# Attention of the last two batches in chunks of 32 queries and 64 keys on quarters and eighths of the matrix array

## The chip, the core and the metric

The kernel runs on one core of a Trainium2 chip. The core has a matmul engine (PE, with its weight loads shown apart as PEld), three engines for elementwise work (DVE, ACT and POOL) and a queue engine SP that only issues transfers. Data lies in on-chip memory of 128 partitions; matmul results go to a second on-chip memory, the accumulator banks. Transfers run on 16 DMA engines, which SP, POOL and ACT feed through queues of their own (q1, q0 and q10 in the profile). The metric is device time in microseconds.

## What is computed

Four batches, 8 heads, 768 positions, 64 numbers per head. Attention works in chunks of 32 queries; each sees 8 memory keys of its head, its own 32 keys, 16 keys to the left and 8 to the right:

```python
for c in range(nc):                       # nc = 768 / 32 = 24
    l_start = max(0, c_start - 16); r_end = min(S, c_start + 32 + 8)
    k_full = concat([mem_k, k[:, :, l_start:r_end]]); v_full = concat([mem_v, v[...]])
    a = exp(q_c @ k_full.T / 8 - max); a = a / (sum(a) + 1e-9)
    out[:, :, c_start:c_end] = a @ v_full
x = out.transpose(0, 2, 1, 3).reshape(B, S, 512)
u = x + real(fft(fft(x, axis=1), axis=2))
un = (u - mean(u)) / sqrt(var(u) + 1e-6)
out = u + relu(un @ w_ch1) @ w_ch2        # 512 -> 2048 -> 512
```

So a chunk needs 8 + 16 + 32 + 8 = 64 keys.

## The kernel before

Each batch goes through three parts: attention (`attention`, two heads at a time, four pairs a batch, 16 pairs n = 0 to 15), a Fourier part with sums and statistics (`fourier`, `columns_of`), and an MLP (`mlp`, three blocks of 256 rows, each with a first layer L775 and a second layer L793; in batches 2 and 3 the second layer is made from seven half-size products, L842).

**Attention of a pair.** q and k come through POOL's queue with a cast to bf16 (`e_load_qk`, L345 and L349). For batches 0 to 2 PE turns them (L377) and ACT or DVE copies the result out (L395, L420). For batch 3 they are loaded row by row and turned by a DMA transpose from SP (`e_flip_q`, `e_flip_k`), and DVE copies windows of k from `kU` into `kTb` (L415). `kTb` holds 12 blocks of 128 columns: 32 empty ones, 8 memory keys (L408) and 88 keys around a block of 64 queries. Scores (L433) are made in two groups of six blocks; the two heads lie in the two row halves of the array:

```python
nc.tensor.matmul(sc[:, hh, t6, :], kT[r0:r0 + 64, t, :], qT[r0:r0 + 64, ts(t, 64)],
                 start=True, stop=True, tile_position=(r0, 0))
```

A block of 64 queries holds two chunks with different keys, so two exponentials per group (L441) add a bias `mbias` that removes the keys of the other chunk. The values `va` (L358, L362, L367: seven transfers by SP a pair) have the same 128-row blocks and a 65th column of ones, which gives the sum of the exponentials. Value matmuls (L457) are float32, two groups of 12, into two banks `xa` and `xo`; the two blocks of 64 queries lie in the two column halves of the array. A float32 matmul shows as two records. DVE divides by the sum (`e_norm`, L467 and L468) into the batch's buffer `xsb`, of which there are three; batch 3 uses batch 0's again.

**The order of the work.** Nothing is scheduled on the chip. `Plan.order` (L92) walks through a list of tasks while the program is built: each has an engine, a cost, predecessors (`after`, `behind`), buffers that it takes and gives back, and for transfers a size (`moved`, `grain`). It writes one fixed order for each engine. MLP tasks have the lowest priority and fill PE where nothing else is due. On the chip every engine and queue works in that order and waits where something is not ready. SP's queue carries the v loads, the turning of the Fourier rows through DRAM (L567, L568, read back by POOL, L572), the transposes of the MLP's input (`e_flip`, L748), those of batch 3's q and k, and the stores (L856, L859, L866).

## Time and profile before

| | |
|---|---|
| median of 3 runs | 281.31 us (281.21 to 281.39) |
| the profiled execution's own time | 282.55 us |
| its span, first to last instruction | 280.7 us |
| PE busy, granted clock | 264.3 us, 1.0 throughout |
| DVE, ACT, POOL busy | 193.5, 155.2, 64.3 us |
| scores: L433, 384 matmuls | 11.5 us on PE |
| values: L457, 768 records | 28.8 us on PE |
| exponentials: L441, 64 | 33.6 us on ACT, 0.576 us each |
| q and k loads of batch 3: 16 of 96 KB | 8.9 and 9.5 us from issue to landing |

A line of the profile names a source line, an engine, what is written and read, and how often. In a chain line the numbers are the start and the length of a piece, both in microseconds; "x12" counts matmuls, or records where a float32 matmul has two. PE's records overlap, since a matmul takes some 0.2 us from first to last number while the next starts earlier, so the length of a piece of many is read from the chain. Rows by stage give the stage, its length, the busy time of PE, PEld, DVE, ACT and POOL with their instructions, the granted clock, the mean busy share of the 16 DMA engines and GB/s.

### The profile page before, as it was taken

How to read it: one execution, taken by the hardware profiler on the slowest of the kernel's cores; microseconds unless marked ns; L12 is line 12 of the kernel's file. 1: busy time of each engine (PE TensorE's matmuls, PEld its weight loads, DVE VectorE, ACT ScalarE, POOL GpSimd, SP SyncE). 2: the span in 40 equal slices, each digit the busy share in tenths (PEclk: the TensorE clock that was granted, in tenths of full speed). 3: DMA queues.
4: the chain of work that ended last, by engine and by line, in shares of the span. 5: the costliest groups of instructions: out<-in, count | busy, mean ns of one | idle time of the engine just before them, and what ended most of it. 6: DMA issues, size and time to landing. Idle time of an engine off the chain costs nothing.

```text
span 280.7 us, 7981 instructions
## 1 busy us (share of the span) xinstructions
PE 264.3 (94%) x3325; PEld 207.4 (74%) x3325; DVE 193.5 (69%) x424; ACT 155.2 (55%) x262; POOL 64.3 (23%) x127
## 2 busy tenths in 40 slices
PE   0589999999999999998999999999999999999995
PEld 0466698788756579766668766858988888888884
DVE  7968978970218979899688776599869825353444
ACT  6887667579665757734745665525526270605150
POOL 8840853240111038306200230101004100000000
PEclk9999999999999999999999999999999999999999
DMA  6989999999899969999999734497101507103152
GB/s 102 199 143 174 162 206 204 196 198 201 162 190 236 214 103 220 177 142 144 235 191 209 177 74 109 108 207 167 48 37 58 131 21 168 40 37 77 50 103 76
DMA packets 116116, 39.98 MB, mean 142 GB/s; under 512 B 104560, under 2 KB 111472, under 8 KB 116080
## 3 DMA queue, kind: packets, MB, share of 16 engines
q1 hardware_dynamic: 93888, 23.54, 46.9%
q0 software_dynamic: 21472, 15.21, 34.0%
q10 hardware_dynamic: 720, 0.72, 0.7%
q8 instruction: 26, 0.43, 0.7%
q14 instruction: 10, 0.08, 0.1%
HBM read 37.36 MB, written 13.37 MB: 181 GB/s over the span
## 4 chain that ended last, share of the span: by engine, by line
PE 84%; DMA 7%; DVE 4%; SPq 3%; issue 1%; POOL 0%; POOLq 0%
PE ph L775 31%; PE pc L793 15%; PE pc L842 13%; DMA va<-in_v_dram 6%; PE ps L529 6%; PE xa L457 4%; PE pm L699 4%; PE ps L688 3%; PE xo L457 3%; PE sc L433 2%; SPq L358 2%; DMA qs<-in_q_dram 1%; PE trk L377 1%; PE trq L377 1%; DVE xsb L705 1%; PE pm L580 1%
## 5 line engine op out<-in xcount | busy, mean ns | idle before, releaser
L775 PE MATMUL ph<-unT,w_sb 128*128 128x256 f16 x768 | 90.3, 273 | 0.8 <-DVE xsb L800 0.8
L784 ACT ACTIVATE hT<-ph 128x512 f16<-128x512 f32 x96 | 56.9, 598 | 54.3 <-PE pc L842 30.2
L775 PEld LDWEIGHTS <-w_sb 128*128 128x128 f16 x768 | 73.2, 98 | 11.1 <-issue 1.7
L793 PE MATMUL pc<-w_sb,hT 128*128 128x512 f16 x192 | 44.8, 380 | 0.0
L441 ACT ACTIVATE e<-sc,mbias 128x384 f32<-128x384 f32 x64 | 33.6, 576 | 19.0 <-PE sc L433 19.0
L793 PEld LDWEIGHTS <-hT 128*128 128x128 f16 x192 | 17.7, 98 | 19.0 <-issue 0.2
L847 DVE TENSOR_TENSOR xsb<-pc,xsb 128x256 f32<-128x256 f32 x43 | 18.0, 421 | 12.4 <-PE pc L842 10.6
L842 PEld LDWEIGHTS <-hT 128*128 128x128 f16 x240 | 23.3, 98 | 4.2 <-DVE hT L830 1.0
L842 PE MATMUL pc<-w_sb,hT 128*128 128x256 f16 x192 | 24.1, 272 | 0.5 <-DVE hT L830 0.5
L541 ACT CAST up<-ps 128x386 f16<-128x386 f32 x16 | 9.7, 605 | 17.6 <-PE ps L529 17.0
L830 DVE TENSOR_TENSOR S<-hT 128x768 f16<-128x768 f16 (+1 forms) x12 | 5.1, 422 | 18.5 <-ACT hT L784 17.9
L800 DVE SCALAR_TENSOR_TENSOR xsb<-pc,rstd,xsb 128x512 f32<-128x512 f32 x12 | 9.0, 750 | 12.2 <-PE pc L793 12.1
L713 DVE BATCH_NORM_STATS2 st<-xsb 128x6 f32<-128x512 f32 x24 | 16.6, 690 | 0.6
L705 DVE TENSOR_TENSOR xsb<-pm,xsb 128x512 f32<-128x512 f32 x15 | 10.2, 678 | 7.1 <-PE pm L699 6.9
L457 PEld LDWEIGHTS xa<-va,e 128*64 128x64 f32 x384 | 12.5, 137 | 3.2 <-issue 2.0
L457 PE MATMUL xa<-va,e 128*64 128x65 f32 x384 | 14.7, 226 | 0.0
L433 PEld LDWEIGHTS <-kTb 64*128 64x128 bf16 x384 | 7.8, 96 | 9.0 <-issue 8.1
L457 PE MATMUL xo<-va,e 128*64 128x65 f32 x384 | 14.1, 223 | 0.0
L546 DVE TENSOR_TENSOR up<-ps,up 128x386 f16<-128x386 f32 x16 | 9.6, 602 | 6.1 <-ACT up L541 6.1
L395 ACT COPY qT<-trq 128x768 bf16<-128x768 bf16 x12 | 9.5, 793 | 6.4 <-PE trq L377 6.4
L572 POOL DMA_DIRECT2D xr<-x_back x3 | 2.3, 770 | 46.7 <-DMA x_back<-x_rows 46.7
L519 DVE TENSOR_TENSOR lo<-ff,hi 128x768 f16<-128x768 f32 x12 | 11.3, 954 | 2.4 <-ACT hi L514 2.4
(168 smaller groups left out, 455.3 us busy)
## 6 DMA issues: line engine op xcount, KB each, us to landing
va<-in_v_dram SPq DMA_DIRECT2D x32, 220.0 KB
w_sb<-in_moe_w_ch_dram POOLq DMA_DIRECT2D x8, 512.0 KB, 16.9
out_dram<-xsb SPq DMA_DIRECT2D x12, 256.0 KB
qs<-in_q_dram POOLq DMA_DIRECT2D x12, 192.0 KB, 6.5
ks<-in_k_dram POOLq DMA_DIRECT2D x12, 192.0 KB, 7.0
x_rows<-xsb POOLq DMA_DIRECT2D x3, 768.0 KB, 4.6
xr<-x_back POOLq DMA_DIRECT2D x3, 768.0 KB, 5.0
out_rows<-xsb SPq DMA_DIRECT2D x9, 256.0 KB
```

Of the source, the lines that this page charges most:

```text
L433: nc.tensor.matmul(sc[:, hh, t6, :], kT[r0:r0 + 64, t, :], qT[r0:r0 + 64, ts(t, 64)], start=True, stop=True, tile_position=(r0, 0))
L441: nc.scalar.activation(e1[:, :, :, ts(half, 32)], sc[:, :, 0:6, ts(half, 32)], AFT.Exp, bias=mbias[:, half:half + 1], scale=1.0 / math.sqr ...
L457: nc.tensor.matmul(xa[64 * half:64 * half + 64, st, hh, 0:65], e1[:, hh, t6, :], v1[:, hh, 6 * g + t6, 0:65], start=True, stop=True)
L519: nc.vector.tensor_tensor(lo[:, ab].rearrange(fl), ff_of[b, par][:, ab].rearrange(fl), hi[:, ab].rearrange(fl), ALU.subtract)
L529: nc.tensor.matmul(out_[:, sp, :], part[:, ab, sp * 3 + st, c0:c1], tab[:, sp, st, :], start=(st == 0 and i == 0), stop=(st == 2 and i == 1))
L705: nc.vector.tensor_tensor(uv, pm_of[b, kt], uv, ALU.add)
L713: nc.vector.bn_stats(st6, xs[b][:, kt, :])
L775: nc.tensor.matmul(ph[:, k, :], w1_sb[:, dt, ts(HH * k + i, P)], unT_of[b, j][:, dt, :], start=(dt == 0), stop=(dt == NDT - 1))
L784: nc.scalar.activation(hT_of[b, j][:, :, i, :], ph, AFT.Relu, bias=0.0, scale=1.0 if b in EVEN else -1.0)
L793: nc.tensor.matmul(pc_of[b, j, r], hT_of[b, j][:, k, i, ts(r, P)], w2_sb[:, HH * k + i, :], start=(i + k == 0), stop=(i + k == HH))
L842: nc.tensor.matmul(pc_of[key], a[:, i, :], w[:, i, :], start=(i == 0 and new), stop=(i == HH - 1), skip_group_check=not new)
L847: nc.vector.tensor_tensor(u, pc, u, ALU.add)
```

## The change

For pairs n >= 8 (batches 2 and 3) a chunk of 32 queries gets a block of its own with exactly its 64 keys, so the exponential needs no mask. `kTb` is then read as 24 blocks of 64 columns. Scores are 48 matmuls of 32 columns, each on one quarter of the array (64 rows by 64 columns): the row half is the head, the column half alternates with the chunk. Values are 48 float32 matmuls on eighths (64 rows by 32 columns): the row half is where the chunk's exponentials lie, the column quarter is the chunk's place in a tile of 128 queries, so the result comes out as 128 queries by 6 tiles for one head, one head in `xa` and one in the other bank. One exponential replaces four. The `va` buffers get the new layout: 12 transfers a pair, with the memory rows in both halves, and once for each of four buffers the ones column and empty edges are written again by ACT (`e_recast`), from a pattern that POOL makes at the start (`e_edge`).

Batch 3's q and k are cast once, whole, from DRAM to DRAM by two POOL transfers (`e_cast`), behind batch 1's read-back; SP then loads them in bf16 row by row (16 transfers).

The planner changes too: costs and transfer sizes of tasks are new; idle times of ACT and DVE overlap a little (`OVER`); SP holds back after a large transfer until 2.2 us before its end by the model (`ROOM`); dependencies of reused buffers are written out (`t_used`); and the list of tasks is ordered 25 times, 24 of them with ranks moved at random for tasks after the first Fourier part, keeping the order with the earliest modelled end (`shortest`). So the order of all engines' work differs, the first part aside. The loads of v for pairs 14 and 15 come behind batch 2's row turning.

```diff
+    OVER = {"DVE": 0.08, "ACT": 0.1}
+    lead = 0
+    ROOM = 2.2
...
+    def shortest(self, tries, spread):
+        free, ranks = dict(self.free), [t["rank"] for t in self.tasks]
+        found = None
+        for i in list(range(tries)) + [None]:
+            draw = random.Random(found[1] if i is None else i)
...
+                t["rank"] = rank if even or rank < self.lead or rank > 1e5 else rank + move
...
+            placed = self.order()
+            if found is None or self.end < found[0]:
+                found = (self.end, i)
+        return placed
...
-                if idle.get(e, 0.0) > now:
+                if idle.get(e, 0.0) > now or (e == "SP" and self.full and self.full["done"] - self.ROOM > now):
...
+    NCH = S // CHUNK
+    FINE = 8
...
+    def e_edge():
+        nc.gpsimd.memset(edge, 1.0)
+        for p0, hh, t, i in EDGES:
+            ones = edge[p0:p0 + 32, i:i + 1]
+            nc.gpsimd.affine_select(out=ones, in_=ones, compare_op=ALU.is_ge, fill=0.0, ...)
+            if i == 0:
+                nc.gpsimd.memset(edge[p0:p0 + NMEM, i:i + 1], 1.0)
+
+    def e_recast(i):
+        v1 = va[i]
+        nc.scalar.activation(v1[:, :, :, D], strided(mhalf, 0, [[0, 2], [0, NT]]), AFT.Copy, scale=-2.0)
+        for p0, hh, t, j in EDGES:
+            nc.scalar.copy(v1[p0:p0 + 32, hh, t, 0:D], zero[p0:p0 + 32].to_broadcast([32, D]))
+            nc.scalar.copy(v1[p0:p0 + 32, hh, t, D:D + 1], edge[p0:p0 + 32, j:j + 1])
...
+    half_qk = nc.dram_tensor("half_qk", [2, H, S, D], BF16).ap()
+
+    def e_cast(i):
+        rows = [x.rearrange("h s d -> (h s d)").rearrange("(e r c) -> e r c", e=16, c=2048)
+                for x in (half_qk[i], (q, k)[i][TURNED])]
+        nc.gpsimd.dma_start(*rows)
...
-                nc.gpsimd.dma_start(
+                nc.sync.dma_start(
                     strided(dst[n % NS], hh * D, [[2 * D, NST], [1, D]]),
-                    src[b, 2 * pr + hh].rearrange("(a p) d -> p a d", p=P))
+                    half_qk[i, 2 * pr + hh].rearrange("(a p) d -> p a d", p=P))
...
+        if n >= FINE:
+            for hh in range(2):
+                lo, hi = 64 * hh + NMEM, 64 - 64 * hh + NMEM
+                run(lo, WIN, 1, NT - 1, 64 - LEFT, hh)
+                run(hi, WIN, 0, NT - 1, CHUNK - LEFT, hh)
+                run(lo + LEFT, WIN - LEFT, 0, 1, 0, hh)
+                run(hi, WIN - RIGHT, NT - 1, 1, S - CHUNK - LEFT, hh)
+                for half in range(2):
+                    nc.sync.dma_start(v1[64 * half:64 * half + NMEM, hh, :, 0:D],
+                                      mem_v[b, 2 * pr + hh].unsqueeze(1).to_broadcast([NMEM, NT, D]))
+            return
...
+    def half_of(c, hh):
+        return 64 * ((c + hh) % 2)
+
+    def f_scores(n):
+        qT, kT = qT_of[n], kTb[n % NKT].rearrange("p t (h k) -> p (t h) k", h=2)
+        sc_of[n] = sc = aps.tile([P, 2, 16, CHUNK], FP32, tag="sc", bufs=1, name="sc")
+        for c in range(NCH):
+            for hh in range(2):
+                r0, p0 = 64 * hh, half_of(c, hh)
+                nc.tensor.matmul(sc[p0:p0 + 64, hh, c // 2, :], kT[r0:r0 + 64, c, :],
+                                 qT[r0:r0 + 64, ts(c, CHUNK)], start=True, stop=True,
+                                 tile_position=(r0, p0))
+
+    def f_exp(n):
+        sc = sc_of.pop(n)
+        e1_of[n] = e1 = apool.tile([P, 2, NT, CHUNK], FP32, tag="e1", bufs=3, name="e1")
+        nc.scalar.activation(e1, sc[:, :, 0:NT, :], AFT.Exp, scale=1.0 / math.sqrt(D))
+
+    def f_values(n):
...
+        for c in range(NCH):
+            for hh in range(2):
+                p0, c0 = half_of(c, hh), CHUNK * (c % 4)
+                nc.tensor.matmul(xa[hh][c0:c0 + CHUNK, c // 4, 0:65],
+                                 e1[p0:p0 + 64, hh, c // 2, :], v1[p0:p0 + 64, hh, c // 2, 0:65],
+                                 start=True, stop=True, tile_position=(p0, c0))
...
+        if n == TURNED * HP:
+            t_cast.extend(add("POOL", 1.0, lambda i=i: e_cast(i), moved=2.6, grain=0.2, late=1.0,
+                              behind=t_xr[1]) for i in range(2))
...
+        if FINE <= n < FINE + NV:
+            t_ones[n] = add("ACT", 1.0, lambda: e_recast(n % NV), [t_used.get(("va", n % NV)), t_edge, t_zero])
+        lv = add("SP", 2.5, lambda: e_load_v(n), [t_ones.get(n), t_used.get(("va", n % NV))],
...
+        if fine:
+            t_used["kTb", n % NKT] = t_sc[n, 0] = s_ = add(
+                "PE", 0.40, lambda: f_scores(n), [eq, ek], take=("sc",), give=("qT", "kTb"))
+            x_ = t_exp[n, 1] = add("ACT", 0.98, lambda: f_exp(n), [s_], take=("e1",), give=("sc",))
+            vp = pick_of["v", n] = dict(of=("mlp", "acc"))
+            v_ = add("PE", 0.8, lambda: f_values(n), [x_, lv], take=("xa",), pick=vp, give=("e1", "va"))
...
+    t_lv[14]["behind"] = t_lv[15]["behind"] = [t_x2[TURNED - 1]]
...
-        for t in plan.order():
+        for t in plan.shortest(24, 1.5):
```

## The prediction

> **What bounds the kernel now.** I read the page first: busy shares, slices, chain. Then the table by stage, the chain in order of time where batch 2's attention runs, a close window on single matmuls, and the DMA queues.

> From the page (busy time, slices, chain, queues):

> ```profile
> span 280.7 us, 7981 instructions
> PE 264.3 (94%) x3325; PEld 207.4 (74%) x3325; DVE 193.5 (69%) x424; ACT 155.2 (55%) x262; POOL 64.3 (23%) x127
> ...
> PE   0589999999999999998999999999999999999995
> ...
> DMA  6989999999899969999999734497101507103152
> ...
> q1 hardware_dynamic: 93888, 23.54, 46.9%
> q0 software_dynamic: 21472, 15.21, 34.0%
> ...
> PE 84%; DMA 7%; DVE 4%; SPq 3%; issue 1%; POOL 0%; POOLq 0%
> ```

> The matmul engine (PE) never rests after slice 4 and makes 84% of the chain. The DMA engines are as full until about 160 us.

> The stages in which batches 2 and 3 run:

> ```profile
> 100.00:120.00 20.00, 20.00 (x292) 16.39 (x292) 16.51 (x34) 12.86 (x23) 10.68 (x13) 1.00 1.37 178
> 120.00:140.00 20.00, 19.19 (x176) 12.93 (x174) 16.53 (x33) 10.59 (x17) 6.63 (x7) 1.00 1.43 173
> 140.00:160.00 20.00, 20.00 (x243) 15.32 (x242) 15.64 (x30) 10.37 (x19) 1.25 (x3) 1.00 1.10 196
> 160.00:180.00 20.00, 20.00 (x279) 14.21 (x277) 12.46 (x31) 11.58 (x20) 3.63 (x11) 1.00 0.44 98
> ```

> PE is idle 0.81 us in 80; ACT has 7 to 10 us of 20 free in each, DVE 3 to 8. The last but one column is the DMA share (over 1 where packets of two queues overlap): no room before 160 us, half a stage after.

> The chain around batch 2, and the end of batch 3's Fourier part and the start of its MLP:

> ```profile
> 98.70 0.28 PE sc L433 x12
> 98.99 0.47 PE trk L377 x16
> 99.46 0.97 PE pc L793 x4
> ...
> 103.41 0.28 PE sc L433 x12
> 103.70 0.98 PE ph L775 x8
> 104.68 0.85 PE xa L457 x24
> 105.53 0.70 PE xo L457 x24
> 106.22 1.85 PE ph L775 x16
> ...
> 214.17 0.87 PE pm L699 x8
> ...
> 236.83 0.87 PE ph L775 x8
> ```

> An attention piece costs its own time plus 0.11 us on the piece behind it: L793 x4 takes 0.97 here and 0.86 elsewhere, L775 x8 0.98 and 0.87.

> How many run at once, from windows that cut a piece after its first matmuls:

> ```profile
> 98.64 0.20 PE L433 MATMUL sc<-qT,kTb 64*128 64x64 bf16 x2
> ...
> 104.61 0.28 PE L457 MATMUL xa<-va,e 128*64 128x65 f32 x2
> ```

> Two scores (two row halves) start within 0.03 us and two value matmuls (two column halves) within 0.02 us, each lasting 0.2 us or more. So the array runs as many at once as it has parts: two.

> **The change part by part.** The sum is made on the profiled execution: span 280.7 us, own time 282.55 us, 1.24 above the median of 281.31. I take the difference off the median.

> *Scores, PE.* Before, a pair of heads needs two groups: 2 x (0.28 + 0.11) = 0.78 us. A group without about 0.11 us of switching is 0.17 us, six rounds of two, 29 ns a round for 64 columns. After: one piece of 48 matmuls of 32 columns on four quarters, 12 rounds. If a round scales with its columns it is 15 ns, 0.18 + 0.22 = 0.40 us; if it keeps 29 ns, 0.35 + 0.22 = 0.57; if only two run at once, 24 rounds, 0.70 + 0.22 = 0.92. I take 0.57, since 29 ns is the shortest round that the trace shows: 0.21 less.

> *Values, PE.* Before: 0.85 + 0.70 + 0.11 = 1.66 us. The second half is clean: 24 records, 12 rounds of two, 58 ns; the first carries 0.15 of entry. After: 48 float32 matmuls, 96 records of the same 65 columns. On eight parts 12 rounds, 0.70 + 0.15 + 0.11 = 0.96; four at once 24 rounds, 1.66, nothing gained; two at once 48 rounds, 3.04. I take 0.96, because both kinds of halves filled up in the trace: 0.70 less.

> Together 0.91 us a pair, 7.3 us for eight pairs. Bounds: (0.38 + 0.70) x 8 = 8.6 us less; two at once, (0.14 + 1.38) x 8 = 12.2 us more.

> [...] The rows above show overlap of two; no trace here shows four or eight.

> *ACT.* Four exponentials of 0.576 us become one of 128x768; rows of 768 and 1056 elements took 0.793 and 1.037, so about 0.85: 1.45 less a pair. The copy of k on 1344 elements instead of 1056 costs some 0.25 more for batch 2's four pairs. New are nine small copies for each of four va buffers at about 0.2 (small copies in the trace: 0.195 to 0.204), 7 us. Net 3 to 4 us less on an engine 55% busy: no effect on the end, 0; cover is the 7 to 10 us free in each stage. If the cover fails at a buffer's turn, values wait up to 1.8 us.

> *DVE.* Norms keep their 384 elements. The copy of kU grows from 0.422 to about 0.53 us four times, the memory-key copy from 96 to 192 elements: under 1 us, behind 3 to 8 us free a stage: 0.

> *POOL.* Seven small mask operations (rows of 0.09 to 0.27) are 1.3 us, written before a gate copy that waits 9.6 us for va: 0; without that cover 1.3. Sixteen q and k issues of 0.84 us leave POOL, two casts come; they stand behind batch 1's mirror load. POOL is 23% busy.

> *DMA and SP.* va: 7 transfers and 2,256 rows of 256 B a pair become 12 and 3,024; 6,144 more packets. One of q1 costs 46.9% x 16 x 280.7 / 93,888 = 22.4 ns, so 8.6 us of all sixteen engines; five more issues of 0.3 us a pair, 12 us of SP's queue. Batch 3's 12,288 rows of q and k go from q0 to q1, counted even, 16 more issues (5 us of SP). The casts write 1.57 MB; q0 moved 15.21 MB in 34.0% of the span, 0.159 MB/us: 10 us. So 19 us more of DMA. Today there is no room before 160 us, so batch 3's attention, which ends at 179, moves out by up to 19. What hides that is 21.8 us: batch 3's last columns end at 215.0 and its MLP starts at 236.8, PE having older MLP work meanwhile.

> *Waits added or moved.* The order written for the changed kernel uses that slack up. Between batch 3's last-row matmuls and its first MLP matmul stand 16 first-layer, 8 column and 56 product matmuls, 1.75 + 0.87 + 6.12 = 8.7 us. In the trace batch 1 needs 10.4 us for that stretch (last row done at 118.5, MLP at 128.9, third transpose issued at 126.3). So PE may wait 1.7 us; I take 1.5. All six stores of batch 0 now stand on SP behind batch 3's last loads and flips; the first norm of batch 3 waits for them, the values of the next pair wait for that norm's bank, and PE's order is fixed, so what stands behind waits too. A row of such a store is 0.4 us to issue; I count 0 since SP's work falls due near there, but up to 6 us if SP is late.

> *The new order elsewhere.* SP's first 57 transfers are unchanged and first values wait for them, so the first 33 us keep their time: 0, within 0.5. Batch 0's sums and statistics now come ahead of batch 1's first norm on DVE; PE's waits there are 0.65 us in all, so between 0.65 less and 1 us more; 0.

> Sum: -7.3 + 1.5 = -5.8 us; 281.3 - 5.8 = 275.5 us.

> **The rivals.**

> *A. No wait:* everything lands in time and rounds of scores shrink with their columns. 281.3 minus 7.3 to 8.6: 272.7 to 274.0 us. For: PE waited only 0.81 us in those stages under a fixed order. Against: 8.7 us against 10.4.

> *B. Half the gain:* values run four at once, so 1.7 us is left, 279.6 us before waits; or waits of 3 to 6 us, 278 to 281. For: no row shows both kinds of halves together. Against: nothing limits either kind in the trace.

> *C. SP becomes the bound (slower):* one mechanism at one place. SP runs in order and carries 17 us more of issues and 19 us of DMA demand. Batch 3 comes later than the written order expects, PE stands at the second values of batch 3 (about 180 us) with older MLP work queued behind. Its price is each us of lateness one for one; it decides above 7.3 us. At 12 us late: 281.3 - 7.3 + 12 = 286 us. For: 0.44 and 0.75 of DMA share after 160 us already. Against: q0 carries less there and the 21.8 us.

> *D. Parts do not run at once (also slower):* the change doesn't do what it says; 281.3 + 12.2 = 293.5 us.

> **How the numbers follow.** Main case (274.0 to 278.0) 0.50; A 0.17; B 0.16; C 0.11; D 0.04; within 0.2% 0.02. About 0.2%, 0.56 us, is what can be told from no change here. Faster: 0.50 + 0.17 + 0.16 = 0.83; same 0.02; slower 0.15. The range goes from 272.0, inside A, to 281.5, over B: it leaves out some 0.03 below and 0.15 above. The likeliest case's own range is 274.0 to 278.0.

> **What would show it.** Right: a score piece of 48 at 0.4 to 0.6 us and a values piece of 96 records at 0.85 to 1.0 with its exit; PE's busy time about 7 us lower; PE idle under 3 us between 100 and 240 us; batch 3's last columns near 222. Wrong: values at 1.5 us or more (B, D); PE waiting several us for a va load, a flip, or a norm held by stores (C); an idle first 33 us.

## The result, and the profile after

The changed kernel takes 297.27 us (median of six runs, 296.20 to 299.73); the kernel before 281.88 us (median of six). The ratio is 1.0556, with a 95% interval of 1.0521 to 1.0592: 5.6% slower, some 15.6 us, where 275.5 us and at most 281.5 were predicted. The profiled execution took 299.73 us, the longest of the six and 2.46 us above the median; its span is 298.0 us, 17.3 more than the span before. Ratios here and below are of the fast runs of a kernel, which leaves out those more than 1.5% above its fastest: two of the kernel before (286.49 and 284.91 us), two of four with the stores ahead (297.66 and 298.14) and one of four with both edits (298.37).

The page of the changed kernel (busy time, slices, granted clock, queues, shares of the chain):

```profile
span 298.0 us, 9167 instructions
PE 267.1 (90%) x3898; PEld 207.5 (70%) x3898; DVE 193.9 (65%) x424; ACT 152.2 (51%) x274; POOL 53.2 (18%) x120
...
PE   0689999999995999999999999266999998999995
...
PEclk9999999999998999999999999958899999999999
DMA  6999999999999996579979359794494421313152
...
q1 hardware_dynamic: 113056, 26.69, 50.2%
q0 software_dynamic: 9024, 15.21, 25.5%
q8 instruction: 30, 0.49, 0.7%
...
PE 13%; DMA 1%; DVE 0%; issue 0%
```

The chain is followed back only to 252 us, so its shares say little here.

PE, which hardly rested from slice 4 to the last, now has three holes: a slice of 5 near 90 us, slices of 2, 6 and 6 from 186 us on, and an 8 near 250 us. Behind the first two the granted clock falls, to 0.91 in the mean of the 20 us from 80 on, 0.84 from 180 and 0.91 from 200. Where it is at half, a 128x256 matmul of L888 starts 213 ns after the one ahead of it, elsewhere 109. So PE's busy time, 2.8 us more than before, holds work done at half speed, and says nothing yet of the matmuls saved. The stages (us, PE, PEld, DVE, ACT, POOL busy, granted clock, DMA share, GB/s):

```profile
80.00:100.00 20.00, 16.71 (x406) 9.95 (x408) 13.17 (x20) 10.54 (x21) 0.80 (x1) 0.91 1.03 168
100.00:120.00 20.00, 20.00 (x424) 15.67 (x412) 17.03 (x35) 9.77 (x16) 1.84 (x3) 1.00 0.85 192
...
160.00:180.00 20.00, 20.00 (x310) 13.14 (x309) 5.04 (x13) 10.22 (x16) 2.88 (x7) 1.00 0.60 101
180.00:200.00 20.00, 11.93 (x238) 8.08 (x239) 6.89 (x14) 3.56 (x6) 0.00 (x0) 0.84 0.90 229
200.00:220.00 20.00, 17.34 (x334) 14.16 (x327) 14.43 (x32) 5.32 (x10) 0.84 (x1) 0.91 0.70 137
```

What PE waited for (total us, times, longest):

```profile
PE xa L534 <- DVE xsb L545: 7.8, 1, 7.8
...
PE trq L447 <- issue: 3.3, 1, 3.3
PE xa L534 <- issue: 2.0, 1, 2.0
PE pc L955 <- DVE xsb L960: 1.4, 3, 0.7
PE pc L955 <- DVE hT L943: 1.1, 3, 0.4
...
PE xo L534 <- issue: 0.4, 1, 0.4
```

**The stand of 7.8 us.** The values of batch 3's second pair wait for the first norm of batch 3. DVE has computed the reciprocals at 186.50 and multiplies at 195.34, when the stores of batch 0 have left the buffer; SP issues those stores right after the last k flip:

```profile
186.50 0.19 DVE L544 RECIPROCAL zs<-xa 128x6 f32<-128x6 f32 x1
195.34 0.56 DVE L545 TENSOR_TENSOR xsb<-xa,zs 128x384 f32<-128x384 f32 x1 [8.65 <-DMA out_dram<-xsb]
```

```profile
188.13 1.23 SPq L456 DMA_TRANSPOSE kU<-ks  x1
189.42 4.10 SPq L969 DMA_DIRECT2D out_dram<-xsb  x7
```

**The stops put down to "issue".** PE stops in the middle of pieces, with no wait in sight. Here between the second and the third of sixteen transposes:

```profile
88.32 0.56 PE L518 MATMUL sc<-qT,kTb 64*64 64x32 bf16 x48
88.81 1.04 PE L906 MATMUL pc<-w_sb,hT 128*128 128x512 f16 x4
89.78 0.23 PE L447 MATMUL trq<-ident_b,qs 96*64 96x96 bf16 x2
93.28 0.49 PE L447 MATMUL trq<-ident_b,qs 96*64 96x96 bf16 x14 [3.27 <-issue]
```

The page has a queue q8 of the kind "instruction": 30 packets of 16,384 bytes, one for each 260 or so of PE's 7,796 recorded instructions. One of them runs from 90.50 to 91.87 us, inside this hole, and PE goes on 1.41 us after it. The hole of 2.05 us at 205.0 ends 1.46 us after another (204.32 to 205.60), the one of 0.37 at 201.3 ends 1.57 us after one that landed at 200.12.

**The sum.** From 33 us to its last matmul PE is idle 17.0 us, before it was 2.0: 7.8 for the stores, 5.7 in the stops put down to issue (3.27 + 0.37 + 2.05), 2.1 between the products of the MLP, 1.4 in small ones. The clock is at half from 94.5 to 97.9, 193.5 to 200.3 and 207.1 to 210.5 us; PE works 11.2 us of that time, which costs 5.6, an estimate that takes half of it as lost, from steps of 213 and 426 ns at half clock (L888 and L906) where 109 and 216 were measured elsewhere. The added idle time and the half clock are 15.0 + 5.6 = 20.6 us, the span grew by 17.3, so the matmuls themselves got some 3 us shorter.

### The profile page after: what moved, and what is told of

Read it like the earlier page. It is cut to its first block, busy times and chain, and to the rows that moved or that the text cites. A ratio compares the mean times of both kernels' runs of the same rounds, so it can differ in the third digit from the quotient of the medians.

```text
span 298.0 us, 9167 instructions
## 1 busy us (share of the span) xinstructions
PE 267.1 (90%) x3898; PEld 207.5 (70%) x3898; DVE 193.9 (65%) x424; ACT 152.2 (51%) x274; POOL 53.2 (18%) x120
## 3 DMA queue, kind: packets, MB, share of 16 engines
q1 hardware_dynamic: 113056, 26.69, 50.2%
q0 software_dynamic: 9024, 15.21, 25.5%
## 5 line engine op out<-in xcount | busy, mean ns | idle before, releaser
L888 PE MATMUL ph<-unT,w_sb 128*128 128x256 f16 x768 | 91.8, 276 | 0.4 <-ACT hT L897 0.3
L888 PEld LDWEIGHTS <-w_sb 128*128 128x128 f16 x768 | 74.4, 99 | 12.6 <-issue 1.8
L906 PE MATMUL pc<-w_sb,hT 128*128 128x512 f16 x192 | 46.5, 390 | 0.0
L906 PEld LDWEIGHTS <-hT 128*128 128x128 f16 x192 | 18.0, 100 | 20.0 <-issue 2.0
L554 ACT ACTIVATE e<-sc,mbias 128x384 f32<-128x384 f32 x32 | 16.8, 582 | 5.4 <-PE sc L505 5.3
L534 PE MATMUL xa<-va,e 64*32 64x65 f32 x384 | 10.6, 237 | 9.8 <-DVE xsb L545 7.8
L534 PEld LDWEIGHTS xa<-va,e 64*32 64x32 f32 x384 | 8.8, 110 | 11.8 <-DVE xsb L545 8.5
L943 DVE TENSOR_TENSOR S<-hT 128x768 f16<-128x768 f16 (+1 forms) x12 | 5.0, 420 | 15.9 <-ACT hT L897 15.5
L627 ACT CAST hi<-ff 128x768 f16<-128x768 f32 x12 | 9.8, 832 | 9.7 <-DVE ff L619 9.6
L837 ACT ACTIVATE un<-xsb,rs 128x512 f16<-128x512 f32 x12 | 9.2, 806 | 6.6 <-POOL rs L852 6.6
L955 PE MATMUL pc<-w_t,S 128*128 128x256 f16 x96 | 11.8, 272 | 0.9 <-DVE xsb L960 0.9
L478 DVE COPY kTb<-mkT 128x192 bf16<-128x192 bf16 (+1 forms) x15 | 3.7, 256 | 13.3 <-PE sc L505 9.3
```

The source lines that it names most:

```text
L534: nc.tensor.matmul(xa[hh][c0:c0 + CHUNK, c // 4, 0:65], e1[p0:p0 + 64, hh, c // 2, :], v1[p0:p0 + 64, hh, c // 2, 0:65], start=True, stop= ...
L554: nc.scalar.activation(e1[:, :, :, ts(half, 32)], sc[:, :, 0:6, ts(half, 32)], AFT.Exp, bias=mbias[:, half:half + 1], scale=1.0 / math.sqr ...
L627: nc.scalar.copy(hl_of[b, par][0][:, ab].rearrange(fl), ff_of[b, par][:, ab].rearrange(fl))
L888: nc.tensor.matmul(ph[:, k, :], w1_sb[:, dt, ts(HH * k + i, P)], unT_of[b, j][:, dt, :], start=(dt == 0), stop=(dt == NDT - 1))
L906: nc.tensor.matmul(pc_of[b, j, r], hT_of[b, j][:, k, i, ts(r, P)], w2_sb[:, HH * k + i, :], start=(i + k == 0), stop=(i + k == HH))
L955: nc.tensor.matmul(pc_of[key], a[:, i, :], w[:, i, :], start=(i == 0 and new), stop=(i == HH - 1), skip_group_check=not new)
```

## The experiments

**What a fine pair costs (f1).** Repeats of fine pieces with other sizes and another order:

```diff
+        if n in (8, 9, 10, 11):      # values of 12 to 15 likewise, w = 65, 32, 16, 65
+            if n == 11: todo.sort(key=lambda x: (x[1], half_of(*x)))
+            w = (32, 16, 8, 32)[n - 8]
+            for c, hh in todo:
+                nc.tensor.matmul(sc[p0:p0 + 64, hh, c // 2, 0:w], ...)
```

> Repeats of fine pieces, each writing again values that it has just written (so the output stays): scores of pairs 8 to 11 again with 32, 16 and 8 columns, and with 32 columns sorted so that matmuls of the same part of the array follow each other; values of pairs 12 to 15 again with 65, 32 and 16 columns, and with 65 sorted by part. Theory R of the prediction (rounds on parts): scores a round of four, 29 ns, with columns maybe less; values 12 rounds of 58 ns on eight parts, so half the columns give about half of 1.1 us, and sorted by part they take several times 1.1 us. Theory I (PE starts one matmul each 10 to 11 ns, whatever its size; 48 scores took 0.49 us, 96 records of values 1.11 us): the repeats take 0.49 and 1.0 us with any number of columns, and only the sorted ones are longer.

Measured (313.90 us with the repeats), from the start of a piece to the start of the next, gaps left out, and the mean step between starts:

```
scores again, 32 columns          0.55 us     7.8 ns
scores again,  8 columns          0.47 us     7.8 ns
scores again, 32, sorted by part  1.44 us    25.0 ns   (median 31)
values, 65 columns                1.11 us    10.1 ns a record
values again, 65 columns          1.07 us    10.0 ns
values again, 65, sorted by part  4.48 us    44.2 ns   (median 56)
at half clock: values 65 columns 15.5 ns; 32 columns 11.4; 16 columns 11.4
```

Sorted by part, a record of the values starts 56 ns (median) after the one ahead of it, near the round of 58 that the prediction took. Unsorted, a record starts each 10 ns, more than five in the 56 ns that one takes on a single part: so the parts do run at once, though not at the 58/8 = 7.3 of eight full rounds. At full clock the step of the scores does not shrink with the columns (7.8 ns with 8 and with 32; values with fewer columns ran only at half clock). Theory I holds at full clock as far as this was measured; at half clock 65 columns step by 15.5 ns and 32 or 16 by 11.4, so there the columns count, as R says. A pair's pieces are 0.49 + 1.11 us, and with the 0.11 us that each piece adds to the next one (L906 x4 took 0.97 us behind the scores at 88.3 us, 0.87 at 149.0) 1.82, against 0.56 + 1.55 + 3 x 0.11 = 2.44 before: 0.62 less a pair, 5.0 us for eight.

**Instruction fetch, in the kernel before (b1).** Bunches of extra small matmuls:

```diff
+        for _ in range({8: 4, 9: 8, 10: 16, 11: 32, 12: 8, 13: 16, 14: 32, 15: 24}.get(n, 0) * (g == 1)):
+            for t6 in range(6):          # 12 matmuls of one column, over values just written
+                ...
```

> The kernel before, with extra matmuls of one column behind the second scores of each pair of batches 2 and 3, which write again what stands there: 48, 96, 192 and 384 in batch 2 (while the DMA engines are full), 96, 192, 384 and 288 in batch 3. Each is two instructions of PE, and a packet of the instruction queue (16 KB) is fetched for each 250 or so of them. Theory F: up to 96 cost 8 to 10 ns each; at 192 and more PE stops in the middle of the piece for 1 to 4 us until about 1.4 us after such a packet has landed, at 384 twice or more; and the clock falls to half after it. Without F: 8 to 10 ns each throughout, 0.5, 1, 2 and 4 us, and no gap.

Measured: 328.64 us. Each extra matmul took 13.3 to 14.3 ns, not 8 to 10 (two halves of the array here, not four quarters). Bunches of 48 and 96 have no gap. The 192 have one each, 5.11 us in batch 2 and 1.32 in batch 3; the 384 two each, 3.6 and 3.0 us in sum; the 288 two, 2.5 us. All eight end 1.31 to 1.51 us after a packet of the instruction queue has landed, and the clock is at half for 6.8 or 10.2 us in or behind each of these five bunches. Where a bunch has two stops, they lie 128 matmuls apart, which is 256 instructions, about what a packet holds. The longest one:

```profile
107.35 0.31 PE L441 MATMUL sc<-qT,kTb 64*128 64x1 bf16 x14
112.77 0.22 PE L441 MATMUL sc<-qT,kTb 64*128 64x1 bf16 x4 [5.11 <-issue]
```

Theory F holds for the gaps, and not for the 8 to 10 ns: nothing but more instructions in a row was added.

**Instruction fetch by itself (m1).** A kernel that leaves the whole computation out: 60 wide matmuls, a bunch, 60 more, with and without transfers beside it.

```diff
+        for n in (48, 96, 144, 192, 256, 384):
+            bunch(n)        # 64x64 parts, 32 columns
+            fill(60)        # 128x128, 512 columns
```

> A kernel that leaves the whole computation out and writes zeros: PE runs 60 matmuls of 512 columns (13 us), then a bunch of small tiled matmuls (64 by 64, 32 columns, two instructions each), six times, with bunches of 48, 96, 144, 192, 256 and 384; first with no other transfers, then the same while SP's queue moves 256-byte rows. Theory F: bunches up to 96 or 144 run at 8 to 10 ns a matmul without a gap; from 192 on PE stops in the middle of the bunch until about 1.4 us after a 16 KB packet of the instruction queue. If the fetch suffers from other transfers, as the 5.1 us gap among full DMA engines against 1.3 to 2.1 us elsewhere suggests, the gaps of the second half are longer by 1 us or more; if it does not, both halves show the same gaps. Without F: no gaps.

Measured: no gap up to 192, in either half (without transfers the slope from 48 to 192 is 8.3 ns a matmul; with them the 192 take 0.19 us longer). At 256 one gap, 2.01 us without and 2.75 with transfers; at 384 two, 2.14 + 2.24 without and 3.89 + 2.18 with. The two stops of a bunch again lie 128 matmuls apart. The limit is higher than expected, for a reason that no run shows. The other transfers add 0.7 to 1.7 us to the gaps of a bunch.

```profile
74.82 0.36 PE L71 MATMUL tiny<-wide 64*64 64x32 bf16 x23
77.20 0.53 PE L71 MATMUL tiny<-wide 64*64 64x32 bf16 x45 [2.01 <-issue]
```

```profile
180.32 0.54 PE L71 MATMUL tiny<-wide 64*64 64x32 bf16 x40
183.61 0.29 PE L71 MATMUL tiny<-wide 64*64 64x32 bf16 x13 [2.75 <-issue]
```

**The stores ahead (s1).**

```diff
+        placed = moved(t_early, t_flips[2][0], before=True)   # t_early: the six stores of batch 0
```

> The six stores of batch 0 move in SP's queue from behind batch 3's last k flip to ahead of batch 2's first flip of un; nothing else is reordered. Theory W (the stores hold the first norm): in the changed kernel's trace PE stands from 188.16 to 195.95 us until that norm, 7.8 us, and the clock is at half until 200.3 us, which costs another 2.2 us. Both go, 10 us; the next thing late is the last k flip (its copy on DVE at 196.5 us), which may take back up to 3.5. So 287 to 291 us. Theory S (SP as a whole is late, 20 us behind the written order by the last loads): whatever of batch 3 comes next is as late as the stores were, and the time stays at 294 to 297 us.

Measured: ratio to before 1.0405 (1.0327 to 1.0482), about 293.3 us; the stores' stand is gone, and 4 us came back, not 10. The waits of PE in its place:

```profile
PE sc L518 <- DVE kTb L485: 3.3, 1, 3.3
PE xo L534 <- issue: 1.8, 1, 1.8
...
PE trq L447 <- issue: 1.4, 1, 1.4
```

The scores of batch 3's third pair now wait for their k, whose flip SP issues at 178.3 us as it did before the move (178.0). The result lies between the theories: the stores' place was the cause of that stand, and right behind it stands SP.

**The fine pieces apart (s2).**

```diff
+        placed = moved([t_sc[9, 0], t_exp[9, 1]], pe(t_sc[9, 0], 4))
+        far = pe(t_used["v", 15], 3)
+        placed = moved([t_used["v", 15], t_norm[15, 0], t_norm[15, 1]], far)
+        placed = moved([t_used["v", 14], t_norm[14, 0], t_norm[14, 1]], pe(t_used["v", 14], 2))
```

> The order of PE alone changes (with the exponential and the norms that hang on the moved pieces): the scores of the second pair of batch 2 come three pieces later than the values of the first, and batch 3's last two values pieces stand two and three pieces further apart. Theory F (instruction fetch): the trace shows PE idle for 3.27 us at 90.0 in the middle of 16 transposes, and for 0.37 and 2.05 us at 201.3 and 205.0 in the middle of values pieces, each ending 1.4 us after a 16 KB packet of the instruction queue has landed; a fine pair is 288 instructions in 1.6 us and was 144. Spread out, the gaps go, 5.7 us, and with them the half clock after them, 3.4 us: 288 to 291 us, and a stand at about 188 us for the norm as before. Theory D (PE waits there for data or a buffer that comes at the same time anyway): the gaps stay in other places, 296 to 299 us.

Measured: 297.92 us, ratio 1.0548 (1.0492 to 1.0605), nothing gained. Yet the stops put down to issue went from 5.7 to 1.0 us, as F says. The half clock did not go with them: it is 13.7 us in both kernels, now behind waits for data:

```profile
PE xa L534 <- DVE xsb L545: 6.3, 1, 6.3
PE pm L812 <- DVE xsb L702: 3.8, 1, 3.8
PE pc L955 <- DVE xsb L960: 2.7, 4, 1.3
...
PE xa L534 <- issue: 1.0, 1, 1.0
```

PE comes 2.6 us earlier to batch 2's first column products (149.0 us, in the changed kernel 151.6) and then waits 3.8 us for a bank: the sum that frees it waits for batch 2's mirrored rows, which SP's queue turns through DRAM and POOL reads back, at 150.25 us (in the changed kernel at 150.37). The third column product runs at 158.2 us, in the changed kernel at 157.0. So both theories were half right: F for the cause of the stops, D for the time.

**Both edits (s3).**

> Both edits together, the stores ahead and the fine pieces apart. If W and F both hold and the losses are separate, 297.3 - 10 - 9.1 = 278 us, up to 283 with the last k flip late. If S holds, 285 to 289; if D holds, 287 to 291; if neither W nor F, 295 or more.

Measured: ratio 1.0306 (1.0211 to 1.0400), about 291 us; lowest run 289.32. That is above what S gave and within the range of D. The profile is of the longest run, 298.37 us, so the waits are those of that run:

```profile
PE sc L518 <- DVE kTb L485: 6.0, 2, 3.1
PE pm L812 <- DVE xsb L702: 3.4, 1, 3.4
```

With the stores out of the way and the stops small, PE waits for the flips of the last two pairs and for the mirror, which all go through SP. The losses are not separate: one hides the next.

**The parts of the change.** Attention of before with casts and new order (p2), fine attention with loads of before (p1), and the new order alone (p3):

```diff
-    FINE = 8
+    FINE = 16                      # p2 and p3: old attention
-                nc.sync.dma_start(..., half_qk[i, 2 * pr + hh]...)
+                nc.gpsimd.dma_start(..., src[b, 2 * pr + hh]...)   # p1 and p3: old loads
```

> Attention and loads of before with the planner's new costs, its room rule for SP and its search: what the new order is worth alone. The prediction counted it at 0 (0.65 less to 1 more): 280.7 to 282.5 us. In the changed kernel's trace the products of the MLP wait 2.1 us on DVE that they did not wait before; if that belongs to the order, 283 to 285 us; if the place of batch 0's stores in the order also makes PE stand here, 287 us or more.

> Another part undone: batches 2 and 3 use the attention of before; the casts and the planner's new costs and search stay. PE gets 5 us of matmuls back; SP loses 40 issues of va for eight pairs (some 15 us before batch 3's end) and the DMA engines 6,144 packets; PE's instructions of a pair fall from 288 to 144. Theory F+S: no gaps in the middle of pieces and no stand for the stores; 281.5 + 2 for the products of the MLP = 282 to 286 us. If the stand of PE comes from the casts or from the order as written, 292 us or more.

> One part of the change undone: batch 3's q and k come from float32 in DRAM through POOL's queue as before; fine attention and the planner's new costs and search stay. Theory S (SP is as much the bound as PE from 80 to 200 us: it issues for 88 of 100 us from 100 on; the sixteen loads from the casts take 0.79 us of SP each, 12.6 us in all, where the prediction put 5): SP comes that much earlier to the stores of batch 0 and the last flips, the stand of 7.8 us and its half clock go, the fetch gaps stay: 286 to 290 us. Theory W (only the place of the stores counts, not the load on SP): the stores are still written behind the last flips and the time stays at 294 to 298 us.

Measured; beside it, from the traces, the time that SP spends on issues that begin from 100 to 200 us and when it issues the last k flip:

```
                      median us   ratio to before          SP issues  last k flip
before                                                     64.0 us    160.7
new order alone       281.06     0.9955 (0.9928-0.9982)    59.7       168.6
order + casts         289.53     1.0266 (1.0207-1.0325)    71.0       176.1
order + fine          291.99     1.0323 (1.0251-1.0395)    72.5       179.0
order + casts + fine  297.27     1.0556 (1.0521-1.0592)    88.4       188.1
```

Each of these kernels has an order of its own, since the search runs anew over the tasks that are left. SP issues the six stores of batch 0 at 105.9 to 131.5 us with the order alone; with the casts two of them come behind the last flip (177.3 and 178.0), with the fine attention all six. So a difference between two rows holds such places in the order too.

The order costs nothing by itself; it is the one part that gains, 0.45%, within the 2% that count as the same. Its page shows PE full:

```profile
span 279.1 us, 7968 instructions
PE 265.2 (95%) x3322; PEld 208.9 (75%) x3322; DVE 193.1 (69%) x424; ACT 154.4 (55%) x262; POOL 64.4 (23%) x134
...
q1 hardware_dynamic: 93888, 23.54, 44.7%
q0 software_dynamic: 21472, 15.21, 33.6%
```

The casts cost 3.1 points on it, the fine attention 3.7, both 6.0. What the casts cost is not work of the DMA engines, of which there is less: q1 and q0 take 44.7% and 33.6% of 279.1 us with the order alone, 218.5 us, and 46.5% and 26.5% of 289.5 us with the casts, 211.3 us. With the casts the stores' stand is there without any fine attention, so F+S was wrong for p2: the order puts the last two stores of batch 0 behind the flips, and the norm waits 10.4 us:

```profile
169.91 0.19 DVE L581 RECIPROCAL zs<-xa 128x6 f32<-128x6 f32 x1
180.53 0.56 DVE L582 TENSOR_TENSOR xsb<-xa,zs 128x384 f32<-128x384 f32 x1 [10.44 <-DMA out_dram<-xsb]
```

With the old loads the stand is gone, though the stores are written behind the last flip there too: SP issues them from 180.2 us on, 9 us earlier than in the changed kernel, and DVE does not wait for them. So S holds against W for the stand; the time lies 2 us above the range that S gave. What is left in p1:

```profile
PE ph L888 <- ACT hT L897: 4.5, 7, 1.1
PE trk L447 <- issue: 2.1, 1, 2.1
PE ph L888 <- issue: 2.0, 1, 2.0
```

Two stops put down to issue, each followed by 3.4 us of half clock, which costs 1.7; and 4.5 us in which first-layer pieces wait for the one bank that is free. Two banks hold batch 2's column products until the mirror is there (its last transfer is issued at 159.1 us, 16.6 later than with the order alone, and DVE waits 7.8 us for it), a third the values of batch 3's first pair, whose norm is written for after the stores. Against 5 us of matmuls saved that is a loss.

Two kernels were planned behind these and have no measurement. One is fine attention with the old loads, its pieces apart and the mirror ahead; by p1's sum it could come to 292 - 4.1 - 3.4 - 4.5 = 280 us, an estimate. The other is p2 with the stores ahead. Without it, it stays open how the 8.5 us between p2 and the order alone divide: PE's wait for the two late stores is 5.8 us of them, and whether it comes from their place in the order or from SP's load is not told apart there.

## Why the prediction was wrong

- **What failed first: the step on DMA and SP.** It priced batch 3's sixteen loads from the casts at 5 us of SP and let 21.8 us of slack hide 17 us of issues. They took 12.7 us (0.79 each), the issues that begin in the 100 us before 200 take 88.4 us where they took 64.0, and the last k flip comes 27 us later than before. p1, without these loads, has it 9 us earlier and no stand for the stores. The other half of the step, 19 us more work for the DMA engines, did not come: q1 and q0 took 46.9% and 34.0% of 280.7 us before, 227.1 us, and 50.2% and 25.5% of 298.0 us after, 225.6 us.
- **The stores of batch 0** were named as behind batch 3's last flips, with the norm and the values of the next pair behind them, and counted at 0, "up to 6 us if SP is late". They cost 7.8 us and 2.2 of half clock. This is rival C word for word, at the second values of batch 3 (188 us where about 180 was said); its price, "one for one", left out the clock. C had a chance of 0.11; it should have been more, since the prediction named the place and had shown no slack on SP itself. s1 gave back 4 of the 10 us: behind the stores the flips are late too.
- **No term for instruction fetch.** The prediction counted instructions as time on PE only. The stops and the half clock behind them are 5.7 + 3.4 = 9.1 us in the profiled run; b1 and m1 show such stops where only more small matmuls were added: 1.32 to 5.11 us in bunches of 192, 2.01 and 2.75 in those of 256. What they cost in the end is less clear: s2 took 4.7 us of them away and gained nothing.
- **Scores and values** were right in kind and mis-sized: scores 0.60 with their exit (0.57 predicted), values 1.22 (0.96), because starts are 10 ns apart and not 7.3. 5.0 us saved, not 7.3. D, that parts don't run at once, is refuted by f1 (10 ns a record, 44 sorted by part).
- **The start of batch 3's MLP**, +1.5: PE had work until the third transpose came. The chain, where it begins:

```profile
252.46 2.30 DMA unT<-un
254.76 0.05 issue
254.81 5.20 PE ph L888 x46
```

  Next to nothing there; but the products before it wait 2.1 us for DVE, which had no term.
- **ACT, POOL and the first 33 us** at 0: right; PE waits at most 1.0 us in all for any group of ACT's, and the one for POOL is 0.9 as in the kernel with the old attention. **The new order** at 0: right, 1.3 us better.

By these terms: -5.0 + 10.0 + 9.1 + 2.1 = 16.2 us of the 17.3 in the span. The terms are read from one trace; s1 and s2 show that they overlap, so they are not what each change would give back.

## What to carry to other kernels

When work moves to a queue, add up that queue's own issue time by stage, at the duration that the trace has for this kind of transfer, before you call it hidden; a slack that was read on another engine does not hide it. When matmuls are cut small, count instructions: PE stopped here in bunches of 192 small matmuls (b1) and of 256 (m1), two instructions each, and not in bunches of 96 (b1) and 192 (m1), and in the changed kernel the half clock behind the stops cost more than half as much again (3.4 us beside 5.7, an estimate). And look for the second loss behind the first: taking away one of them alone gave nothing (s2) or two fifths of its size (s1) here.
